# Attention with a bucket mask on one core: query parts of 256 and 512 columns instead of two of 384

## The chip, the core and the metric

The kernel runs on one core of a Trainium2 chip. The core has five engines with queues of their own: TensorE (PE; its weight loads are shown apart, as PEld), VectorE (DVE), ScalarE (ACT), GpSimd (POOL) and SyncE (SP), which here only issues DMAs. The metric is the time on the device in microseconds, as the median of the runs of one comparison.

## What is computed

The first half is attention over 4 batches, 8 heads, 768 positions and 64 values a head, in which a query sees only the keys that fall into its own bucket. The bucket comes from the signs of six projections. The second half is a gated MLP over the joined heads.

```
q_bits = (einsum('bhsd,dk->bhsk', q, proj) > 0)       # k_bits in the same way
mask = q_bucket[:, :, :, None] == k_bucket[:, :, None, :]
scores = where(mask, scale * q @ k.T, -1e9)
scores = scores - max(scores, -1)
attn = exp(scores); attn = attn / (sum(attn, -1) + 1e-9)
x = attn @ v                                          # (4, 768, 512) after joining the heads
h = gelu(x @ w_in); u, v = halves of h; v_n = layer norm of v * g_ln
out = x + (u * (w_sg @ v_n + b_sg)) @ w_out
```

## The kernel before

**Pairs of heads.** Two heads share the 128 partitions, 64 each, so there are 16 pairs. A matmul over one head's 64 rows uses half of TensorE's array, and the two heads' matmuls stand next to each other in the queue and run side by side; I call two such matmuls a row pair. The 768 queries of a pair are taken in two parts of 384, the 768 keys in six tiles of 128.

**The steps of a pair**, by the name of the function and the lines of the profile:

- `load` brings q, k and v by DMAs from SP.
- `parts` (L475 to L482): TensorE transposes 12 tiles, ScalarE rounds the result to the high part (L479; the queries are scaled here), VectorE takes the low part (L482).
- `features` (L497, L500): three matmuls for 384 columns give the projections, VectorE turns them into large signed constants that make the mask in a matmul.
- `largest` (L517, L524): for a tile of 128 queries and half of the keys a rough score, two row pairs of matmuls, and on VectorE the maximum over 384 keys for each head.
- `shift` (L532 to L545): the maxima of a part become one row of the features: VectorE, a spread over TensorE (L539), two ScalarE copies.
- `weigh` (L561, L567, L573, L582): for a tile of keys four row pairs give the scores of 384 queries (high x high, low x high, high x low, features), ScalarE takes the exponential; after every second key tile comes the product with v (four matmuls of 64 columns, two heads side by side); the exponentials are added up on GpSimd, and on VectorE for one key tile of five.
- `finish` (L598 to L621): the sums over keys by matmuls with ones in four strips of 32 columns, a reciprocal by way of DRAM, the scaling (L619) and the store into `xs`.

The product reads p with one more column of ones, 385 in all, which gives the sum of v. Scores, rough scores, transposes, features, spreads and totals all use the same seven PSUM tiles of one bank, `g0` to `g6`; the product has the eighth bank, `av`. A tile is free again when its readers are done.

**Weights.** Beside the attention, 16 jobs (`weight_job`, L326 to L365) split w_in into a high and a low part: per job one DMA, one GpSimd and one ScalarE operation, and seven on VectorE (L356 to L365).

**The order.** A planner (`Plan`) decides the order before the program is built: every group of instructions has an engine, a cost and a due number (`prio`), and the planner gives each engine the due group that can start earliest. The numbers at the top set these: `AVP` how late a product with v is due after its scores, `AHEAD` how many steps the rough scores are ahead, `WSTEP` and `WP` the distance and start of the weight jobs, `PREP` the start of the next pair's preparation. A pair takes 12 due numbers:

```
p0 = 12 * (n - 1) + PREP
weight_job(plan, w_tile, *job, WSTEP * i + WP)
plan.add(PE, 1.48, prio + AVP, product, p[0] + p[1] + [st.v], [av], form="col")
work = g["c"] + (self.TURN_PE if g["form"] != form else 0.0)
```

The form is the shape in which TensorE's array is used: "row" (64 rows, L517 and L561), "col" (64 columns, L573), 32 columns (L598), or the whole array. The MLP after it (L762, L790, L808, L834) uses the whole array throughout.

Of the kernel before, what the change touches and what calls it, by code (L numbers as in the profile page):

```python
# [21 lines left out]
MLP = {"xl": "POOL", "gm": "DVE", "gl": "POOL", "wg": 398.29, "wo": 46.93, "x": 568.79}  # L22

AVP = 4.5
NAV = 1
S0P = 2.08
AHEAD = 5
PREP, SHIFTP, FINP, WSTEP, WP = -2.61, 0.3, 5.42, 11, 9.29
LOADS = "SP"
ADDS = ["POOL", "POOL", "DVE", "POOL", "POOL"]  # L30


class Plan:
# [8 lines left out]
    TURN_PE = 0.09  # L42
    LANES = 8
    TURN = 4.7

# [56 lines left out]
    def order(self):  # L102
# [32 lines left out]
        while len(out) < len(G):  # L135
# [87 lines left out]
def kernel(  # L223
# [19 lines left out]
    P = 128  # L243
# [13 lines left out]
    MISS = 2.0 ** 33  # L257
    EMPTY = 2.0 ** 32
# [4 lines left out]
    QH2, W6 = SH // 2, SH // 64  # L263
# [12 lines left out]
    nc.vector.memset(ones, 1.0)  # L276
    less = const.tile([P, 1], F32, name="less")
# [36 lines left out]
    msts = [const.tile([P, HT, P], F32R, name=f"m{i}") for i in range(2)]  # L314
    for m in msts:
        nc.vector.memset(m.bitcast(F32), 0.0)
# [100 lines left out]
    if True:  # L417
# [30 lines left out]
        def load(n, prio):
# [11 lines left out]
            st.hi, st.lo, st.ft = ([pool.ring([P, S], F32R, f"{a}{c}{n % 3}") for c in "qk"] for a in ("h", "l", "f"))  # L460
# [5 lines left out]
        def parts(st, s, prio):  # L466

            hh, lo, raw, fac = st.hi[s], st.lo[s], st.raw[s], (SCALE, 1.0)[s]
            for hf in range(2):
                tp = ps_tile()  # L470
                cs = slice(hf * SH, (hf + 1) * SH)

                def tr(tp=tp, hf=hf):
                    for i in range(HT):
                        nc.tensor.transpose(tp()[:, i * P:(i + 1) * P],  # L475
                                            raw()[:, hf * HT + i].rearrange("p j d -> p (j d)"), ident)

                def high(tp=tp, cs=cs):
                    nc.scalar.mul(hh()[:, cs], tp()[:, :SH], fac)  # L479

                def low(tp=tp, cs=cs):
                    nc.vector.scalar_tensor_tensor(lo()[:, cs], tp()[:, :SH], fac, hh()[:, cs].bitcast(F32),  # L482
                                                   op0=ALU.mult, op1=ALU.subtract)

                plan.add(PE, 0.38, prio, tr, [raw, (hh, hf), (lo, hf)], [tp])
                plan.add(ACT, 0.49, prio, high, [tp], [(hh, hf)])
                plan.add(DVE, 0.55, prio, low, [tp, (hh, hf)], [(lo, hf)])

        def features(st, s, prio):
            hh, lo, ft = st.hi[s], st.lo[s], st.ft[s]  # L490
            for hf in range(2):
                cs = slice(hf * SH, (hf + 1) * SH)
                fp = ps_tile()

                def project(fp=fp, cs=cs):
                    for i, (w, x) in enumerate(((pwh, hh), (pwl, hh), (pwh, lo))):
                        nc.tensor.matmul(fp()[:, :SH], w[:, s, :], x()[:, cs], start=(i == 0), stop=(i == 2))  # L497

                def sign(fp=fp, cs=cs):
                    nc.vector.tensor_scalar(ft()[:, cs], fp()[:, :SH], fcol[:, 2 * s:2 * s + 1],  # L500
                                            fcol[:, 2 * s + 1:2 * s + 2], op0=ALU.is_gt, op1=ALU.mult)

                plan.add(PE, 0.58, prio, project, [(hh, hf), (lo, hf), (ft, hf)], [fp])
                plan.add(DVE, 0.67, prio, sign, [fp], [(ft, hf)])

        def largest(st, t, prio):

            hf, i = divmod(t, HT)
            if i == 0:
                st.mx = late.ring([P, 2, HT, 2], F32, "mx", 3)  # L510
            mx, qs = st.mx, slice(t * P, (t + 1) * P)
            sc = [[ps_tile() for j in range(2)] for kh in range(2)]

            def mm(kh):
                for n, x in enumerate((st.ft, st.hi)):
                    for j in range(2):
# [11 lines left out]
        def shift(st, hf, prio):  # L528
# [8 lines left out]
            def spread():  # L537
                for i in range(HT):
                    nc.tensor.matmul(tp()[:, i * P:(i + 1) * P], m()[:, i, :], identr, start=True, stop=True)  # L539
# [351 lines left out]
```

## Time and profile before

| | |
|---|---|
| median of three runs | 809.66 us (808.55 to 814.48) |
| the profiled execution | 808.19 us, span 806.4 us |
| attention, first to last matmul | about 5 to 480 us |
| MLP | about 481 to 806 us |
| granted TensorE clock | 0.998 of full speed |

The span is what the profile covers; the execution's own time has 1.8 us around it. In the rows a start is in microseconds from the start of the span. A timeline row gives the start, the length, the engine, the line, the operation, output and inputs, shapes, and how many instructions it merges; since matmuls are pipelined, the distance of two starts says what a matmul costs, and its length doesn't. A group row ends with count, busy time, mean length in ns, and the idle time before the group with what ended it. The chain is the work that ended last, followed back.

### The profile page before, as it was taken

To read this page: it belongs to the slowest core of one execution; us is meant where nothing else is said; L and a number is where in the kernel's file an instruction comes from. 1 tells how busy PE (TensorE), PEld (TensorE's weight loads), DVE (VectorE), ACT (ScalarE), POOL (GpSimd) and SP (SyncE) were. 2 spreads that over 40 slices of the span, in tenths; PEclk is the share of its full clock that TensorE was granted. 3 is DMA by queue.
4 is the path that set the end of the run, shared out by engine and by line. 5 is a ranking of instruction groups with operands and counts; after the bars stand their busy time and mean duration, and the time that the engine had idled before them with its cause. 6 is when DMAs were issued, how large, how long until landed. Compare 5 with 4: busy or idle time off the path is not lost.

```text
span 806.4 us, 14979 instructions
## 1 busy us (share of the span) xinstructions
PE 787.3 (98%) x5480; PEld 606.8 (75%) x5480; DVE 520.7 (65%) x1137; ACT 384.1 (48%) x863; POOL 387.1 (48%) x398
## 2 busy tenths in 40 slices
PE   7999999999999999999989999899999999999998
PEld 5776666666666666666656658898899889988996
DVE  7988888788878879798789645689124141405130
ACT  2566665655655665566556665623232133213211
POOL 0556666666675575676565885333015112501030
PEclk9999999999999999999999999999999999999999
DMA  6132232223313214313221124620402310040003
GB/s 150 34 83 61 67 101 70 80 78 90 83 64 102 74 52 102 73 53 101 73 64 51 31 79 137 225 80 26 153 5 79 105 52 26 15 131 27 1 1 130
DMA packets 98537, 60.65 MB, mean 75 GB/s; under 512 B 64672, under 2 KB 89376, under 8 KB 98464
## 3 DMA queue, kind: packets, MB, share of 16 engines
q1 hardware_dynamic: 96768, 56.94, 24.6%
q10 hardware_dynamic: 1696, 2.76, 1.0%
q8 instruction: 43, 0.70, 0.4%
q14 instruction: 30, 0.25, 0.1%
HBM read 46.90 MB, written 12.78 MB: 74 GB/s over the span
## 4 chain that ended last, share of the span: by engine, by line
PE 88%; DVE 7%; DMA 2%; POOL 1%; issue 1%; ACT 1%; SPq 0%; DVEq 0%; POOLq 0%; ACTq 0%
PE g L561 17%; PE av L573 15%; PE ps_vs L808 12%; PE ps_o L834 8%; PE g L517 8%; PE ps_h L790 8%; PE ps_h L762 7%; PE g L497 4%; PE g L475 3%; DVE mx L524 3%; PE g L539 2%; PE g L598 1%; PE ps_o L839 1%; DMA q<-in_q_dram 1%; POOL xl L697 1%
## 5 line engine op out<-in xcount | busy, mean ns | idle before, releaser
L582 POOL TENSOR_TENSOR sum<-sum,p 128x384 f32<-128x384 f32 x192 | 196.7, 1046 | 109.7 <-ACT p L567 95.8
L524 DVE TENSOR_REDUCE mx<-g 128x1 f32<-128x384 f32 x384 | 189.1, 549 | 54.4 <-PE g L517 53.8
L567 ACT ACTIVATE p<-g 128x384 f32<-128x384 f32 x384 | 160.4, 495 | 125.0 <-PE g L561 121.6
L573 PE MATMUL av<-p,v 128*64 128x385 f32 x768 | 144.9, 499 | 0.0
L573 PEld LDWEIGHTS av<-p,v 128*64 128x64 f32 x768 | 46.7, 136 | 57.7 <-issue 57.0
L561 PE MATMUL g<-hq,hk 64*128 64x384 f32 x384 | 78.9, 389 | 1.7 <-DVE mx L524 1.5
L517 PE MATMUL g<-fk,fq 64*128 64x384 f32 x384 | 73.3, 352 | 3.6 <-DVE mx L524 3.3
L582 POOL TENSOR_TENSOR sum<-p,p 128x384 f32<-128x384 f32 x64 | 64.2, 1023 | 25.7 <-ACT p L567 25.6
L811 DVE SCALAR_TENSOR_TENSOR gt<-ps_vs,g_col,b_bc 128x384 f32<-128x384 f32 x32 | 19.7, 616 | 79.9 <-PE ps_vs L808 79.8
L561 PEld LDWEIGHTS g<-hq,hk 64*128 64x128 f32 x384 | 38.3, 183 | 43.1 <-issue 22.3
L517 PE MATMUL g<-hk,hq 64*128 64x384 f32 x384 | 68.8, 336 | 0.0
L561 PE MATMUL g<-hq,lk 64*128 64x384 f32 x384 | 67.7, 335 | 0.0
L561 PE MATMUL g<-fq,fk 64*128 64x384 f32 x384 | 67.4, 333 | 0.0
L561 PE MATMUL g<-lq,hk 64*128 64x384 f32 x384 | 67.4, 334 | 0.0
L819 POOL TENSOR_TENSOR gs<-gt,gs 128x384 fp32r<-128x384 f32 x32 | 33.0, 1030 | 70.7 <-ACT gs L816 70.5
L834 PE MATMUL ps_o<-woh,gs 128*128 128x512 f32 x192 | 65.5, 402 | 0.0
L808 PE MATMUL ps_vs<-wgh,zh 128*128 128x384 f32 x192 | 64.2, 334 | 0.0
L808 PE MATMUL ps_vs<-wgh,zl 128*128 128x384 f32 x192 | 64.2, 334 | 0.0
L808 PE MATMUL ps_vs<-wgl,zh 128*128 128x384 f32 x192 | 64.1, 334 | 0.0
L773 POOL TENSOR_TENSOR mv<-mv,epsr 128x1 f32<-128x1 f32 x24 | 16.3, 679 | 99.5 <-DVE mv L772 99.5
L770 DVE BATCH_NORM_STATS2 st<-y 128x6 f32<-128x512 f32 x24 | 16.6, 690 | 67.7 <-ACT y L751 67.7
L517 PEld LDWEIGHTS g<-fk,fq 64*128 64x128 f32 x384 | 39.9, 184 | 18.7 <-DVE mx L524 11.2
(125 smaller groups left out, 1621.1 us busy)
## 6 DMA issues: line engine op xcount, KB each, us to landing
q<-in_q_dram SPq DMA_DIRECT2D x32, 192.0 KB, 3.7
k<-in_k_dram SPq DMA_DIRECT2D x32, 192.0 KB, 3.7
v<-in_v_dram SPq DMA_DIRECT2D x16, 384.0 KB, 3.3
rs<-r SPq DMA_DIRECT2D x64, 96.0 KB, 2.9
xs<-xt SPq DMA_DIRECT2D x32, 192.0 KB, 2.2
x<-xs SPq DMA_DIRECT2D x16, 384.0 KB, 2.9
rx<-xs SPq DMA_DIRECT2D x96, 64.0 KB, 1.9
out_dram<-ob SPq DMA_DIRECT2D x24, 256.0 KB
```

The source lines that it names most:

```text
L497: nc.tensor.matmul(fp()[:, :SH], w[:, s, :], x()[:, cs], start=(i == 0), stop=(i == 2))
L517: nc.tensor.matmul(sc[kh][j]()[:, :SH], x[0]()[row(j), qs], x[1]()[row(j), kh * SH:(kh + 1) * SH], start=(n == 0), stop=(n == 1))
L524: plan.add(DVE, 0.56, prio, lambda j=j, kh=kh: nc.vector.tensor_reduce(mx()[:, kh, i, j:j + 1], sc[kh][j]()[:, :SH], axis=AX.X, op=ALU.max ...
L561: nc.tensor.matmul(sc[i][j]()[:, :SH], x()[row(j), ks], y()[row(j), cs], start=(n == 0), stop=(n == 3))
L567: plan.add(ACT, 0.53, prio, lambda i=i, j=j: nc.scalar.activation(p[i][j]()[:, :SH], sc[i][j]()[:, :SH], AF.Exp), [sc[i][j]], [p[i][j]])
L573: nc.tensor.matmul(av()[row(j), :SH + 1], st.v()[:, j, kt, :], p[i][j](), start=(kt == 0), stop=(kt == NT - 1))
L582: (nc.gpsimd if e == POOL else nc.vector).tensor_add(sums[j](), first()[:, :SH], p[i][j]()[:, :SH])
L762: nc.tensor.matmul(ps(), x()[:, ts_], w[:, c, FH:FF], start=(c == 0 and n == 0), stop=(c == NC - 1 and n == 2))
L790: nc.tensor.matmul(ps()[:, :SH], w[:, c, fs], x()[:, cs], start=(c == 0 and n == 0), stop=(c == NC - 1 and n == 2))
L808: nc.tensor.matmul(vp(), z()[:, t, fs], w()[:, t, cs], start=(t == 0 and n == 0), stop=(t == NT - 1 and n == 2))
L819: nc.gpsimd if e == POOL else nc.vector).tensor_sub(gl()[:, cs], gt(), gh()[:, cs].bitcast(F32)),
L834: nc.tensor.matmul(po(), a()[:, ts_], w()[:, f, :], start=(f == 0 and n == 0), stop=False)
```

## The change

The queries of a pair are taken in a part of 256 and a part of 512. In the first part (`ph` 0) a PSUM tile holds two key tiles by 256 queries, in the second (`ph` 1) one key tile by 512 queries, so that every tile of scores fills its bank; a pair has nine such steps (`NU`) instead of twelve. The rough scores come in nine steps too: 128 queries by 512 keys, and 2 x 128 queries by the last 256 keys. Transposes and features come in three chunks instead of four. The exponential applies the scale (the queries are no longer scaled, and the constants of the mask grow by 8). Products with v come in groups of one and two steps (`GY`) and of three and three (`GX`). In `finish`, the small constant is added on ScalarE with the copy of the sums and not on VectorE (L608 before), the scaling moves to GpSimd, and the addition of the mean of v to VectorE, in one operation with its factor. The planner now has a cost for each change of form (`TURNS`) and prefers to stay in a form (`STAY`); a pair takes 18 due numbers; and most due numbers are new. Cut to its core:

```diff
-MLP = {"xl": "POOL", "gm": "DVE", "gl": "POOL", "wg": 398.29, "wo": 46.93, "x": 568.79}
-AVP = 4.5
+MLP = {"xl": "POOL", "gm": "DVE", "gl": "POOL", "wg": 209.05, "wo": 46.93, "x": 568.79}
+AVP = 4.99
+GY, GX, NPT = (1, 2), (3, 3), 16
-AHEAD = 5
-PREP, SHIFTP, FINP, WSTEP, WP = -2.61, 0.3, 5.42, 11, 9.29
+AHEAD = 8
+PREP, SHIFTP, FINP, WSTEP, WP = -3.85, 0.3, 6.08, 12.04, 25.31
-ADDS = ["POOL", "POOL", "DVE", "POOL", "POOL"]
+ADDS = (["POOL", "POOL"], ["POOL", "POOL", "DVE", "POOL", "POOL"])
...
-    TURN_PE = 0.09
+    TURNS = {"row": 0.2, "col": 0.144, "full": 0.17, "c32": 0.1, None: 0.0}
+    STAY = 2.0
...
+            def rank(n):
+                return G[n]["p"] + (self.STAY if e == "PE" and G[n]["form"] != form else 0.0), n
...
-    QH2, W6 = SH // 2, SH // 64
+    NY = S // 3
+    PHASES = ((0, NY), (NY, S))
+    WIDE = 2 * NY
...
-                    nc.scalar.mul(hh()[:, cs], tp()[:, :SH], fac)
+                nc.scalar.copy(hh()[:, ss, cs], at(tp))
...
+            def mm():
+                for c, t in enumerate(tiles):
+                    qs = slice((t0 + t) * P, (t0 + t + 1) * P)
+                    for n, x in enumerate((st.ft, st.hi)):
+                        for j in range(2):
+                            nc.tensor.matmul(sc[j]()[:, c * NY:c * NY + b - a], x()[row(j), 0, qs], x()[row(j), 1, a:b],
+                                             start=(n == 0), stop=(n == 1))
...
+            kts = (2 * u, 2 * u + 1) if ph == 0 else (u,)
...
+            def mm():
+                for i, kt in enumerate(kts):
+                    ks = slice(kt * P, (kt + 1) * P)
+                    for m, (x, y) in enumerate(((hi, hi), (lo, hi), (hi, lo), (ft, ft))):
+                        for j in range(2):
+                            nc.tensor.matmul(sc[j]()[:, i * w:(i + 1) * w], x()[row(j), 1, ks], y()[row(j), 0, cs], start=(m == 0), stop=(m == 3))
...
-                    plan.add(ACT, 0.53, prio, lambda i=i, j=j: nc.scalar.activation(p[i][j]()[:, :SH], sc[i][j]()[:, :SH], AF.Exp),
+                plan.add(ACT, 0.6, prio, lambda j=j: nc.scalar.activation(p[j]()[:, :, :NY], two(sc[j]()), AF.Exp, scale=SCALE),
...
+                def product():
+                    for x in us:
+                        for j in range(2):
+                            if ph == 1:
+                                nc.tensor.matmul(two(av())[row(j)], st.v()[:, j, x, :], ps[x][j]()[:, :, :NY], start=(x == 0), stop=(x == 5))
+                        for i in range(2 - 2 * ph):
+                            for j in range(2):
+                                nc.tensor.matmul(av()[row(j), :NY + 1], st.v()[:, j, 2 * x + i, :], ps[x][j]()[:, i, :],
+                                                 start=(x == 0 and i == 0), stop=(x == 2 and i == 1))
...
+            def total():
+                for i in range(2 - ph):
+                    for j in range(2):
+                        for a in range(2):
+                            r, c = 64 * j + 32 * a, i * NY + a * h
+                            nc.tensor.matmul(tp()[r:r + 32, :h], ones, sums[j]()[:, c:c + h], start=(i == 0), stop=(i == 1 - ph))
...
-            plan.add(DVE, 0.16, prio, lambda: V.tensor_single_scalar(sq(), sq(), 1e-9, op=ALU.add), [sq], [sq], port=True)
...
-            plan.add(ACT, 0.62, prio, lambda: nc.scalar.mul(e(), e(), vm()[:, 0:1]), [e, vm], [e])
-            plan.add(DVE, 0.56, prio, lambda: V.tensor_mul(xt(), un()[:, :SH], rs()), [un, rs], [xt], port=True)
-            plan.add(POOL, 0.98, prio, lambda: nc.gpsimd.tensor_add(xt(), xt(), e()), [xt, e], [xt])
+            plan.add(POOL, 0.13 + n / 420.0, prio + TAILP, lambda: nc.gpsimd.tensor_mul(xt()[:, :n], un()[:, :n], rs()[:, :n]), [un, rs], [xt])
+            plan.add(DVE, 0.1 + n / 960.0, prio + TAILP, lambda: V.scalar_tensor_tensor(
+                xt()[:, :n], e()[:, :n], vm()[:, 0:1], xt()[:, :n], op0=ALU.mult, op1=ALU.add), [xt, e, vm], [xt], port=True)
...
-            p0 = 12 * (n - 1) + PREP
+            p0 = 2 * NU * (n - 1) + PREP
```

The order that comes out is read from the built program, engine by engine (the lists that the prediction counts in). On TensorE, before, a product with v of four matmuls stands between row pairs (L517 rough scores, L561 scores; `g` are PSUM tiles, `h`, `l` and `f` the high part, low part and features of q and k):

```order
L517 MATMUL g_960_3472<-hk_2_2907,hq_2_2880 128x384
L517 MATMUL g_960_3474<-hk_2_2907,hq_2_2880 128x384
L573 MATMUL av_3427<-p_153,v_2689 64x385
L573 MATMUL av_3427<-p_154,v_2689 64x385
L573 MATMUL av_3427<-p_155,v_2689 64x385
L573 MATMUL av_3427<-p_156,v_2689 64x385
L561 MATMUL g_960_3495<-hq_2_2880,hk_2_2907 128x384
L561 MATMUL g_960_3497<-hq_2_2880,hk_2_2907 128x384
```

Of the change, at the same stage of a pair (L608 the product, L494 transposes, L565 the spread, L514 features):

```order
L494 MATMUL g_736_2706<-ident,q_2337 128x128 x4
L608 MATMUL av_2714<-p_163,v_2103 64x512
L608 MATMUL av_2714<-p_164,v_2103 64x512
L608 MATMUL av_2714<-p_165,v_2103 64x512
L608 MATMUL av_2714<-p_166,v_2103 64x512
L608 MATMUL av_2714<-p_157,v_2103 64x512
L608 MATMUL av_2714<-p_158,v_2103 64x512
L565 MATMUL g_736_2738<-identr,m_151 128x128 x2
L514 MATMUL g_736_2744<-h_2_2703,pwh 128x256
```

Three steps' products stand together, and they stand beside work of the whole array.

On VectorE, before, a weight job (`w`, `wx`, `wy`, `wg` are its tiles) is strewn between maxima (L524, `mx`):

```order
L365 SCALAR_TENSOR_TENSOR wil<-wx_2295,wih 128x256
L356 TENSOR_SCALAR wy_2727<-w_6_2658 128x256
L357 SCALAR_TENSOR_TENSOR wx_2729<-w_6_2658,wy_2727 128x256
L524 TENSOR_REDUCE mx_2745<-g_960_2732 128x1
L524 TENSOR_REDUCE mx_2745<-g_960_2734 128x1
L524 TENSOR_REDUCE mx_2745<-g_960_2753 128x1
L524 TENSOR_REDUCE mx_2745<-g_960_2755 128x1
L619 TENSOR_TENSOR xt_2788<-un_2440,rs_2676 128x384
L359 SCALAR_TENSOR_TENSOR wx_2729<-wg_2748,wx_2729 128x256
```

Of the change, in a pair with weight work (the lines of the job are seven higher, the maxima are L547):

```order
L363 TENSOR_SCALAR wy_2889<-w_8_2570 128x256
L364 SCALAR_TENSOR_TENSOR wx_2891<-w_8_2570,wy_2889 128x256
L366 SCALAR_TENSOR_TENSOR wx_2891<-wg_2615,wx_2891 128x256
L368 TENSOR_SCALAR wy_2889<-wx_2891 128x256
L369 SCALAR_TENSOR_TENSOR wy_2889<-w_8_2570,wy_2889 128x256
L370 TENSOR_TENSOR wx_2891<-wx_2891,wy_2889 128x256
L547 TENSOR_REDUCE mx_2931<-g_736_2916 128x1
L547 TENSOR_REDUCE mx_2931<-g_736_2918 128x1
L547 TENSOR_REDUCE mx_2931<-g_736_2923 128x1
L547 TENSOR_REDUCE mx_2931<-g_736_2925 128x1
```

Six operations of one job stand in a row ahead of four maxima.

More of the change, by code (lines that the diff above doesn't have):

```diff
@@ L464, in load @@
             return st
[L466 to L487, printed above, removed]
@@ L528, in shift, with chunk, parts, at @@
-        def shift(st, hf, prio):
+        def chunk(i):
+            (a, b), (c, d) = PHASES
+            return ((slice(0, 2), slice(a, b), [(0, 0), (1, 0)]), (1, slice(c, d), [(1, 1)]), (0, slice(c, d), [(0, 1)]))[i]
+        def parts(st, i, prio):
+            hh, lo, (ss, cs, keys), tp = st.hi, st.lo, chunk(i), ps_tile()
+            def at(t):
+                return two(t()) if i == 0 else t()[:, :WIDE]
+            def tr():
+                c = 0
+                for s, _ in keys:
+                    for t in range(cs.start // P, cs.stop // P):
+                        nc.tensor.transpose(tp()[:, c:c + P], st.raw[s]()[:, t].rearrange("p j d -> p (j d)"), ident)
+                        c += P
+            def high():
+                nc.scalar.copy(hh()[:, ss, cs], at(tp))
+            def low():
+                nc.vector.tensor_sub(lo()[:, ss, cs], at(tp), hh()[:, ss, cs].bitcast(F32))
+            plan.add(PE, 0.48, prio, tr, [st.raw[s] for s, _ in keys] + [(t, x) for t in (hh, lo) for x in keys], [tp], form="full")
+            plan.add(ACT, 0.6, prio, high, [tp], [(hh, x) for x in keys])
+            plan.add(DVE, 0.69, prio, low, [tp] + [(hh, x) for x in keys], [(lo, x) for x in keys])
@@ L570, in product @@
-            def product():
-                for i, kt in enumerate(two):
-                    for j in range(2):
-                        nc.tensor.matmul(av()[row(j), :SH + 1], st.v()[:, j, kt, :], p[i][j](), start=(kt == 0), stop=(kt == NT - 1))
-            plan.add(PE, 1.48, prio + AVP, product, p[0] + p[1] + [st.v], [av], form="col")
-            for i, kt in enumerate(two):
-                if kt == 0:
-                    continue
-                e = ADDS[kt - 1]
-                for j in range(2):
-                    def add(j=j, i=i, e=e, first=p[0][j] if kt == 1 else sums[j]):
-                        (nc.gpsimd if e == POOL else nc.vector).tensor_add(sums[j](), first()[:, :SH], p[i][j]()[:, :SH])
-                    plan.add(e, 1.01 if e == POOL else 0.55, prio + 0.6, add, [p[i][j]] + ([p[0][j]] if kt == 1 else []),
+            sc, p = [ps_tile() for j in range(2)], [p_tile() for j in range(2)]
@@ L585, in weigh, with add, finish @@
+            if u:
+                e = ADDS[ph][u - 1]
+                for j in range(2):
+                    def add(j=j, e=e, first=st.p[0][j] if u == 1 else sums[j]):
+                        a = first()[:, :, :NY] if u == 1 else two(first())
+                        (nc.gpsimd if e == POOL else nc.vector).tensor_add(two(sums[j]()), a, p[j]()[:, :, :NY])
+                    plan.add(e, 1.35 if e == POOL else 0.62, prio + 0.6, add, [p[j]] + ([st.p[0][j]] if u == 1 else []),
                              [sums[j]], port=True)
-        def finish(st, hf, prio):
+        def finish(st, ph, prio):
@@ L592, in finish @@
             V = nc.vector
             def total():
-                for j in range(2):
-                    for a in range(2):
-                        r = 64 * j + 32 * a
-                        nc.tensor.matmul(tp()[r:r + 32, :QH2], ones, sums[j]()[:, a * QH2:(a + 1) * QH2], start=True, stop=True)
-            plan.add(PE, 0.6, prio, total, sums, [tp])
-            plan.add(ACT, 0.32, prio, lambda: nc.scalar.copy(sm(), tp()[:, :QH2]), [tp], [sm])
-            un = late.ring([P, SH + 1], F32, "un", 3)
@@ new lines, in finish @@
+            plan.add(PE, 0.5, prio, total, sums, [tp], form="c32")
+            plan.add(ACT, 0.25 + h / 1400.0, prio, lambda: nc.scalar.activation(sm()[:, :h], tp()[:, :h], AF.Identity, bias=small[:, 0:1]), [tp], [sm])
+            un = late.ring([P, WIDE], F32, "un", 3)
+            m = n + 1 - ph
+            plan.add(ACT, 0.22 + m / 1400.0, prio - 1, lambda: nc.scalar.copy(un()[:, :m], av()[:, :m]), [av], [un])
+            sd, sb = dram.tile([4, h], F32, name=f"s_{st.n}_{ph}"), plan.buf(f"s_{st.n}_{ph}", 1)
@@ L625 @@
+        NPAIR, NU = B * NP, 9
         sts = {}
```

200 lines of the change are left out of this document (105 added, 95 removed).

## The prediction

> **What bounds the kernel now.** I read the page's totals first, then the chain that ended last, then that chain in order of time, then TensorE's timeline inside one period.
>
> ```profile
> span 806.4 us, 14979 instructions
> PE 787.3 (98%) x5480; PEld 606.8 (75%) x5480; DVE 520.7 (65%) x1137; ACT 384.1 (48%) x863; POOL 387.1 (48%) x398
> PE 88%; DVE 7%; DMA 2%; POOL 1%; issue 1%; ACT 1%; SPq 0%; DVEq 0%; POOLq 0%; ACTq 0%
> ```
>
> TensorE carries 88% of the chain. A busy TensorE isn't one at its peak, so the question is what fills its time. The chain in order of time answers it:
>
> ```profile
> 101.59 1.79 PE g L497 x9
> ...
> 246.23 1.79 PE g L497 x9
> ...
> 394.26 0.73 PE g L497 x3
> ...
> 427.25 1.76 PE g L497 x9
> ```
>
> The features of the next pair (L497) come back pair by pair: 101.59 to 246.23 is five pairs, 144.64 us or 28.93 each. In that stretch the chain has TensorE pieces only, so 28.93 us is what one pair costs TensorE there. From 246.23 to 427.25 six pairs take 181.02 instead of 173.58, so 7.4 us were lost to something else. The window from 100 to 200 us shows how near the others are (busy time of TensorE, its weight loads, VectorE, ScalarE, GpSimd, with counts; then the clock):
>
> ```profile
> 100.00:200.00 100.00, 100.00 (x821) 67.62 (x819) 82.59 (x182) 60.58 (x147) 63.08 (x65) 1.00 0.30 81
> ```
>
> The clock column is 1.00, so the throttle plays no part.
>
> **Inside a period.** TensorE's timeline around one product with v:
>
> ```profile
> 250.20 0.35 PE L517 MATMUL g<-hk,hq 64*128 64x384 f32 x2
> 250.48 1.51 PE L573 MATMUL av<-p,v 128*64 128x385 f32 x8
> 251.92 0.44 PE L561 MATMUL g<-hq,hk 64*128 64x384 f32 x2
> 252.20 0.34 PE L561 MATMUL g<-hq,lk 64*128 64x384 f32 x2
> 252.37 0.34 PE L561 MATMUL g<-lq,hk 64*128 64x384 f32 x2
> ...
> 259.42 0.53 PE L598 MATMUL g<-sum,ones 128*32 128x192 f32 x8
> 259.88 0.44 PE L561 MATMUL g<-hq,hk 64*128 64x384 f32 x2
> ...
> 273.27 0.55 PE L539 MATMUL g<-identr,m 128*128 128x128 f32 x3
> 273.66 0.84 PE L475 MATMUL g<-ident,k 128*128 128x128 f32 x6
> 274.43 0.44 PE L561 MATMUL g<-hq,hk 64*128 64x384 f32 x2
> ```
>
> A pair of row-tiled matmuls (two heads side by side) starts 0.17 us after the one before (252.20 to 252.37; 0.174 over longer runs). Across a change of shape (64 rows, 64 columns, 32 columns, full array; I call it a turn) it is 0.28 from 250.20 to 250.48 and again from 251.92 to 252.20, 0.11 lost each time. The product itself takes 1.44 for 8 records, while a long one shows what its stream needs:
>
> ```profile
> 475.68 4.10 PE L573 MATMUL av<-p,v 128*64 128x385 f32 x24
> ```
>
> The 16 further records cost 4.10 - 1.51 = 2.59, 0.162 each, so 8 need 1.30, and 0.14 more is lost. One product between two row stretches thus loses 0.11 + 0.14 + 0.11 = 0.36, or **0.18 a turn**. The period gives the same from the other side: 48 + 24 row pairs and 12 features at 0.174 are 14.6, 48 product records at 0.162 are 7.8, 12 transposes at 0.128 (273.66 to 274.43) 1.5, 6 spreads at 0.13 (273.27 to 273.66) 0.8, two totals at 0.35 (0.46 less one gap) 0.7: together 25.4. The 3.5 left of 28.93 fall on the 22 turns that the list of a period has: **0.16 a turn**.
>
> **The change part by part.** *Turns.* Over the whole attention the lists have 326 changes of shape before and 220 now. The title says five products with v; the list shows three stretches of 64 columns in a steady pair, where six stood. 106 turns x 0.16 = **-17.0 us**; with 0.18, -19.1, with the bare gap 0.11, -11.7. Number and total columns of scores, maxima, features, transposes, spreads and products stay.
>
> *Widths.* Half of the 384-wide matmuls become 256 wide, half 512. Two 512-wide rows of the MLP:
>
> ```profile
> 485.16 0.39 PE L762 MATMUL ps_h<-wih,xh 128*128 128x512 f32 x1
> 485.39 0.40 PE L762 MATMUL ps_h<-wil,xh 128*128 128x512 f32 x1
> ```
>
> 0.23 for 512 and 0.174 for 384 is 0.45 ns a column in both, so 256 columns should take 0.116 and nothing changes. The other bound is the 128-wide spread at 0.13, which costs far more than its columns: if no issue goes under 0.13, the 672 issues of 256 columns (24 + 12 + 6 in a pair, 16 pairs) add 672 x 0.014 = 9.4. What lies under it are the weight loads:
>
> ```profile
> 260.86 0.19 PEld L561 LDWEIGHTS g<-lq,hk 64*128 64x128 f32 x2
> ...
> 273.27 0.41 PEld L539 LDWEIGHTS g<-identr,m 128*128 128x128 f32 x3 [0.30 <-ACT hq L479]
> ```
>
> Two half-height loads together take 0.19, no more than one, and three full ones 0.41, so a further load costs (0.41 - 0.19) / 2 = 0.11, just under 0.116. I take **+2**, bounds 0 and +9.4. The Trainium skill (TensorE: Matmul & The Clock Gate, LDWEIGHTS) says that a load takes columns / 1.2 ns whatever the rows, an estimate of 107 ns here. By that rule this term would be 0 and the time 2 us less; the 0.11 of the trace agrees.
>
> *Totals (L598).* 2 x 192 columns become 256 + 2 x 128: 0.7 x 512/384 = 0.93, +0.23 in each of 16 pairs, **+3.7**. They wait for nothing that they didn't wait for before.
>
> *VectorE, and the 7.4 us.* The stall at 284 us in the chain:
>
> ```profile
> 284.40 1.94 DVE mx L524 x4
> 286.35 0.54 DVE wy L356
> ...
> 287.90 1.04 DVE wy L361
> 288.94 0.48 DVE mx L524
> ```
>
> Maxima stand in VectorE's queue behind a weight job (L356 to L365), their PSUM tiles stay taken, and TensorE waits for a tile. In a pair, 24 maxima become 18. Twelve of them took 5.66 in a row, 0.47 each:
>
> ```profile
> 14.12 5.66 DVE L524 TENSOR_REDUCE mx<-g 128x1 f32<-128x384 f32 x12 [0.20 <-PE g L517]
> ...
> L524 DVE TENSOR_REDUCE mx<-g 128x1 f32<-128x384 f32 x384 | 189.1, 549 | 54.4 <-PE g L517 53.8
> L770 DVE BATCH_NORM_STATS2 st<-y 128x6 f32<-128x512 f32 x24 | 16.6, 690 | 67.7 <-ACT y L751 67.7
> L608 DVE TENSOR_SCALAR sq<-sq 128x6 f32<-128x6 f32 x32 | 15.9, 498 | 4.5 <-DMA sq<-s 4.5
> L582 DVE TENSOR_TENSOR sum<-sum,p 128x384 f32<-128x384 f32 x64 | 33.7, 566 | 3.9 <-POOL sum L582 3.6 <-ACT sm L601 0.3
> ```
>
> By the nearest 512-wide row, 0.14 longer than a 384-wide one, a new maximum takes 0.61: 11.0 a pair against 11.3. L608 goes (15.9 / 16 = 1.0), four adds become two of 0.7 (2.1 to 1.4): VectorE loses about 2 us of its 23.9 a pair (82.59 in 100 us). But the weight jobs are put 12.04 apart where a pair takes 18 steps, not 11 in 12: 1.5 jobs a pair instead of 1.1. A job is seven operations of 0.3 to 1.0, about 4 us, so +1.6 a pair until the jobs are done in the 12th; afterwards there are none. So it comes out lighter, but not by much while the jobs last. I take half of the stalls, **-3.5**, bounds 0 and -7.4.
>
> *Start and end.* The first shift waits for 6 maxima of 0.61 instead of 12 of 0.47, 2 us earlier; TensorE still owes the other maxima, so **-1** (0 to -2). At the end the last part has four adds for each head on GpSimd:
>
> ```profile
> L582 POOL TENSOR_TENSOR sum<-sum,p 128x384 f32<-128x384 f32 x192 | 196.7, 1046 | 109.7 <-ACT p L567 95.8 <-DVE sum L582 7.3 <-DVE lk L482 4.2
> L697 POOL TENSOR_TENSOR xl<-x,xh 128x768 fp32r<-128x768 f32 x16 | 30.4, 1913 | 39.4 <-ACT xh L699 39.4
> ```
>
> Between 1.05 and 1.91 a 512-wide add is 1.33; eight and a VectorE pair are 12 us beside about 13 of TensorE's scores and products, and they start 2 to 3 us later: **+1** (0 to +2). GpSimd has 12 adds of 1.33 a pair for 16 of 1.04, so nothing there. ScalarE loses instructions and has 40% idle. The MLP's list for TensorE is the same row for row, including the place of the gate's weights: 0.
>
> **Sum:** -17.0 + 2 + 3.7 - 3.5 - 1 + 1 = -14.8. The profiled execution took 808.19 for its span of 806.4, 1.5 under the median of 809.66; so the span goes to 791.6 and the median to **794.9 us**.
>
> **Rivals.**
> (a) *VectorE takes over (slower).* For ten pairs the weight jobs come 1.5 to a pair, and the new list has six of a job's operations in a row ahead of four maxima, each holding one of seven PSUM tiles, now full banks. The worst period before, by the chain from 394.26 to 427.25, lost 4.06 us. Without my 3.5 for stalls the gain is 11.3. If ten pairs lose L each and the 7.4 go, the change turns to a loss when 10 L exceeds 18.7, at 1.9 a pair; at 3 a pair it is 809.66 - 11.3 - 7.4 + 30 = 821. For it stands L361, 1.04 above (minimum, median and maximum in ns):
>
> ```profile
> L361 DVE TENSOR_SCALAR wy<-wx x16: 279/289/1104, 26.2 to 436.7; 128x256 int32<-128x256 int32 x16
> ```
>
> VectorE already waits there, up to 0.8 us, most of one of GpSimd's adds, and those adds grow by 0.29. Against: VectorE's load falls and TensorE is ahead by more maxima. The Trainium skill (SBUF — State Buffer, Who interferes with whom) says that a VectorE instruction with two SBUF inputs, or in a two-port mode, and a GpSimd instruction exclude each other for the whole instruction. The 1.04 agrees. 10%.
> (b) *Short streams are bound by their loads*, 0.13 for every 256-wide issue: 7.4 more, 802.3. For it the spread's row, against it the paired loads. 12%.
> (c) *The turns go, but their time returns as a wait*, since products now come late and in lumps and the totals wait for GpSimd's sums: 2.2 above today, 811.9. Against it stand GpSimd's 63% and ScalarE's 61% of busy time. 5%.
> (d) *More*: 0.18 a turn and no stalls, 809.66 - 19.1 + 2 + 3.7 - 7.4 - 1 + 1 = 788.9, or less. 13%.
>
> **How the numbers follow.** My case has 60%, and nearly all of it, with (d) and a third of (b), is faster by over 1%, which is about what this measurement can tell from no change (below 801.6): 0.74. Within 1%: the rest of (b), (c) and the edge of mine, 0.16. Slower: 0.10. All low ends together are -19.1 + 3.7 - 7.4 - 2 = -24.8, 784.9; all high ends -11.7 + 9.4 + 3.7 + 2 = +3.4. The range, 785 to 806, leaves out (a) and little else.
>
> **What would show it.** The features' rows should recur every 27.7 to 28.1 us in steady pairs; a product of six matmuls should be followed at once; 256-wide row pairs should start 0.116 to 0.12 apart (0.13 is (b)); the chain between pairs 9 and 15 should hold fewer VectorE pieces. A period above 28.9 with VectorE or ScalarE pieces in it proves me wrong.

## The result: 818.4 us, one per cent slower

| | before | after |
|---|---|---|
| median, 17 runs each | 809.66 us (805.39 to 814.48) | 818.43 us (812.33 to 821.24) |
| ratio, with its 95% interval | | 1.0103 [1.0083, 1.0124] |
| the profiled execution | 808.19 us, span 806.4 | 820.94 us, span 818.8 |
| first matmul of the MLP, start | 481.56 | 493.02 |

The forecast was 794.9 us, 785 to 806. The change made the kernel slower, and it did so before the MLP: there TensorE begins 11.5 us later, and the span is 12.4 us longer. (The two profiled executions lie 2.5 us above and 1.5 below their medians, so they differ by 4 us more than the medians do.) The page of the profile after, in its totals and in the shares of the chain:

```profile
span 818.8 us, 14669 instructions
...
PE 782.7 (96%) x5608; PEld 599.2 (73%) x5608; DVE 539.0 (66%) x962; ACT 359.6 (44%) x703; POOL 370.6 (45%) x334
...
PE 74%; DVE 19%; DMA 2%; issue 2%; ACT 2%; SPq 0%; POOL 0%; ACTq 0%; DVEq 0%
```

TensorE's share of the chain fell from 88% to 74%, VectorE's rose from 7% to 19%, and VectorE is busy 18.3 us longer (539.0 for 520.7) with 175 instructions fewer. The features' rows of the chain in order of time (start, length) tell where:

```profile
102.81 2.31 PE g L514 x12
...
385.55 2.31 PE g L514 x12
...
413.26 2.17 PE g L514 x12
...
441.59 2.31 PE g L514 x12
```

From 102.81 to 385.55 lie nine pairs, 282.74 us or **31.4 each**, where the forecast had 27.7 to 28.1 and the kernel before 28.93. The two pairs behind them, in which no weight job is left, take 27.71 and 28.33, about the forecast's. Against 28.0 the nine lose 3.4 each, 31 us in all.

The same pairs by windows, first of before and then of after (busy time of TensorE, its loads, VectorE, ScalarE and GpSimd with counts; the granted clock; DMA share and GB/s):

```profile
217.30:246.23 28.93, 28.93 (x239) 19.38 (x239) 23.13 (x53) 17.74 (x44) 18.61 (x19) 1.00 0.28 79
```

```profile
195.74:225.73 29.99, 28.38 (x247) 18.50 (x246) 27.81 (x47) 17.27 (x35) 18.43 (x16) 1.00 0.27 73
...
256.98:290.06 33.08, 29.73 (x247) 19.34 (x247) 28.09 (x44) 16.71 (x34) 19.03 (x17) 0.95 0.28 76
...
385.55:413.26 27.71, 27.71 (x247) 18.75 (x248) 20.32 (x35) 15.16 (x30) 16.84 (x14) 1.00 0.31 81
```

VectorE goes from 23.13 to about 28 us a pair with fewer instructions, and TensorE stands still for 1.6 and 3.4 us in the first two. In the second the clock is 0.95 as well. Over all nine pairs, by the same view, TensorE stands still for 19.5 us; most of the rest of the 31 goes with the clock (last section).

### The profile page after: what moved, and what is told of

Same layout as the page of the kernel before. It is cut to its first block, busy times and chain, and to the rows that moved or that the text cites. A ratio compares the mean times of both kernels' runs of the same rounds, so it can differ in the third digit from the quotient of the medians.

```text
span 818.8 us, 14669 instructions
## 1 busy us (share of the span) xinstructions
PE 782.7 (96%) x5608; PEld 599.2 (73%) x5608; DVE 539.0 (66%) x962; ACT 359.6 (44%) x703; POOL 370.6 (45%) x334
## 4 chain that ended last, share of the span: by engine, by line
PE 74%; DVE 19%; DMA 2%; issue 2%; ACT 2%; SPq 0%; POOL 0%; ACTq 0%; DVEq 0%
PE g L593 14%; PE ps_vs L852 11%; PE ps_o L878 8%; PE g L539 7%; PE av L608 7%; PE ps_h L806 7%; PE ps_h L834 6%; PE g L514 4%; PE av L611 4%; PE g L494 3%; DVE m L559 3%; DVE mx L547 2%; DVE mx L549 2%; DVE mx L558 2%; DVE xt L663 1%
## 5 line engine op out<-in xcount | busy, mean ns | idle before, releaser
L598 ACT ACTIVATE p<-g 128x512 f32<-128x512 f32 x288 | 155.7, 600 | 102.5 <-PE g L593 101.7
L620 POOL TENSOR_TENSOR sum<-sum,p 128x512 f32<-128x512 f32 x128 | 159.3, 1264 | 55.9 <-DVE sum L620 32.0
L547 DVE TENSOR_REDUCE mx<-g 128x1 f32<-128x512 f32 x192 | 121.7, 679 | 21.3 <-PE g L539 18.6
L620 POOL TENSOR_TENSOR sum<-p,p 128x512 f32<-128x512 f32 x64 | 85.4, 1354 | 87.4 <-ACT p L598 87.4
L608 PE MATMUL av<-p,v 128*64 128x512 f32 x384 | 89.6, 602 | 0.0
L593 PE MATMUL g<-h 64*128 64x256 f32 (+1 forms) x384 | 76.3, 360 | 5.6 <-DVE mx L547 4.9
L549 DVE TENSOR_REDUCE mx<-g 128x2 f32<-128x512 f32 x96 | 61.9, 684 | 23.9 <-PE g L539 22.0
L539 PE MATMUL g<-f 64*128 64x256 f32 (+1 forms) x384 | 73.2, 366 | 0.8 <-DVE f L519 0.5
L593 PE MATMUL g<-h,l 64*128 64x256 f32 (+1 forms) x384 | 72.1, 342 | 0.0
L593 PE MATMUL g<-l,h 64*128 64x256 f32 (+1 forms) x384 | 71.0, 339 | 0.0
L593 PE MATMUL g<-f 64*128 64x256 f32 (+1 forms) x384 | 70.9, 338 | 0.0
L539 PE MATMUL g<-h 64*128 64x256 f32 (+1 forms) x384 | 68.3, 342 | 0.0
L608 PEld LDWEIGHTS av<-p,v 128*64 128x64 f32 x384 | 24.9, 137 | 43.8 <-issue 41.8
```

Of the source, the lines that this page charges most:

```text
L539: nc.tensor.matmul(sc[j]()[:, c * NY:c * NY + b - a], x()[row(j), 0, qs], x()[row(j), 1, a:b], start=(n == 0), stop=(n == 1))
L547: nc.vector.tensor_reduce(mx()[:, 0, i0 + w, j:j + 1], sc[j]()[:, :WIDE], axis=AX.X, op=ALU.max, negate=True)
L549: nc.vector.tensor_reduce(mx()[:, 1, i0:i0 + 2, j], two(sc[j]()), axis=AX.X, op=ALU.max, negate=True)
L593: nc.tensor.matmul(sc[j]()[:, i * w:(i + 1) * w], x()[row(j), 1, ks], y()[row(j), 0, cs], start=(m == 0), stop=(m == 3))
L598: plan.add(ACT, 0.6, prio, lambda j=j: nc.scalar.activation(p[j]()[:, :, :NY], two(sc[j]()), AF.Exp, scale=SCALE), [sc[j]], [p[j]])
L608: nc.tensor.matmul(two(av())[row(j)], st.v()[:, j, x, :], ps[x][j]()[:, :, :NY], start=(x == 0), stop=(x == 5))
```

## Where the time goes in a pair

I take the pair with 33.08 us. TensorE's timeline (start, length; in brackets the idle time and what ended it), around the spread L565 that turns the shift's row:

```profile
264.59 2.80 PE L608 MATMUL av<-p,v 128*64 128x512 f32 x12
267.32 0.64 PE L640 MATMUL g<-sum,ones 128*32 128x256 f32 x8
270.48 0.63 PE L565 MATMUL g<-identr,m 128*128 128x128 f32 x4 [2.52 <-DVE m L559]
271.04 0.59 PE L539 MATMUL g<-f 64*128 64x512 f32 x2
271.43 0.63 PE L539 MATMUL g<-h 64*128 64x512 f32 x2
```

TensorE waits 2.52 us for `m`, the result of L559. Over the whole trace the view of waits puts 15.7 us in 17 places to this line, the largest that TensorE has for another engine; next come 4.9 us for maxima (L547), which stand behind the shift and the weight work on VectorE. In that stretch VectorE does this:

```profile
265.71 1.57 DVE L369 SCALAR_TENSOR_TENSOR wy<-w,wy 128x256 f32<-128x256 uint32 x1
267.31 0.81 DVE L370 TENSOR_TENSOR wx<-wx,wy 128x256 f32<-128x256 f32 x1
268.05 1.14 DVE L558 TENSOR_TENSOR mx<-mx 128x8 f32<-128x8 f32 x1
269.22 1.11 DVE L559 SCALAR_TENSOR_TENSOR m<-mx 128x8 fp32r<-128x8 f32 x1
```

L558 and L559 are the shift: eight numbers in each partition, and over 1.1 us each. GpSimd at the same time:

```profile
263.95 2.97 POOL L620 TENSOR_TENSOR sum<-p,p 128x512 f32<-128x512 f32 x2 [0.36 <-ACT p L598]
266.88 0.96 POOL L662 TENSOR_TENSOR xt<-un,rs 128x256 f32<-128x256 f32 x1
267.81 2.49 POOL L620 TENSOR_TENSOR sum<-sum,p 128x512 f32<-128x512 f32 x2
```

The pair of additions that starts at 267.81 ends at 270.30, and L559 ends at 270.33. One addition takes about 1.25, so the first ends near 269.1, where L558 ends (269.19). L558 and L559 have both inputs in SBUF, and each is done when an addition of GpSimd is done. The Trainium skill (SBUF — State Buffer, Who interferes with whom) describes it: a VectorE instruction with two SBUF inputs and a GpSimd instruction that reads SBUF exclude each other for the whole instruction. The trace agrees, and shows what a short instruction pays. The groups of VectorE after (count, busy time, mean ns):

```profile
L559 DVE SCALAR_TENSOR_TENSOR m<-mx 128x8 fp32r<-128x8 f32 x16 | 15.2, 952 | 0.6
L558 DVE TENSOR_TENSOR mx<-mx 128x8 f32<-128x8 f32 x16 | 15.2, 950 | 0.1
L559 DVE SCALAR_TENSOR_TENSOR m<-mx 128x4 fp32r<-128x4 f32 x16 | 15.0, 937 | 0.5
...
L558 DVE TENSOR_TENSOR mx<-mx 128x4 f32<-128x4 f32 x16 | 5.3, 329 | 0.5
```

64 instructions cost 50.7 us. Before, by line (minimum, median and maximum in ns):

```profile
L532 DVE TENSOR_TENSOR mx<-mx x32: 124/166/851, 19.8 to 463.6; 128x6 f32<-128x6 f32 x32
...
L533 DVE SCALAR_TENSOR_TENSOR m<-mx x32: 169/170/175, 20.0 to 463.8; 128x6 fp32r<-128x6 f32 x32
```

L533, the twin of L559, never waited: 0.17 us at all 32 places. L532, the twin of L558, stayed within 0.23 us at 30 places and took 0.57 and 0.85 at the other two. At 0.18 each the 64 would be 11.5 us, so 39 us of waiting came into VectorE's queue. Why L533 never waited, VectorE's timeline before shows, and then GpSimd's:

```profile
260.13 0.22 DVE L532 TENSOR_TENSOR mx<-mx 128x6 f32<-128x6 f32 x1
260.38 0.17 DVE L533 SCALAR_TENSOR_TENSOR m<-mx 128x6 fp32r<-128x6 f32 x1
260.46 1.02 DVE L582 TENSOR_TENSOR sum<-sum,p 128x384 f32<-128x384 f32 x2
```

```profile
257.37 1.97 POOL L582 TENSOR_TENSOR sum<-sum,p 128x384 f32<-128x384 f32 x2 [1.08 <-ACT p L567]
259.71 0.61 POOL L358 TENSOR_TENSOR wg<-w 128x256 f32<-128x256 f32 x1 [0.36 <-DMA w<-in_moe_w_in_dram]
261.51 1.05 POOL L582 TENSOR_TENSOR sum<-sum,p 128x384 f32<-128x384 f32 x1 [1.18 <-DVE sum L582]
```

There the shift stands directly ahead of VectorE's own additions L582, and GpSimd's next addition waits for those (1.18 us idle). The shift fell into a gap that its own queue made. In the new order it stands amid weight work, while GpSimd has its additions in a row.

## The experiments

Two theories stood after this reading. A: the shift's two operations wait for GpSimd's additions, and TensorE waits for the shift. B: the weight jobs, six of their operations in a row, hold up the maxima, and so the PSUM tiles. Each expectation says what its theories make of the run. The ratio is always to the kernel before on the same chip.

### The shift as one reduction (e1), and the same in the kernel before (e4)

`mx` gets a third plane that holds the limit; one `tensor_reduce` takes the minimum of the three. A reduction has one input. What changes in the computation: a query whose bucket holds no key gets the limit (2 to the 35th) as its shift, where it got zero. Nothing else moves on any queue.

```diff
...
-            plan.add(DVE, 0.16, prio, lambda: V.tensor_tensor(mx()[:, 0, :nt], mx()[:, 0, :nt], mx()[:, 1, :nt], op=ALU.min), ...
-            plan.add(DVE, 0.16, prio, lambda: V.scalar_tensor_tensor(
-                m()[:, :nt, MROW::BL], mx()[:, 0, :nt], EMPTY, mx()[:, 0, :nt], op0=ALU.is_lt, op1=ALU.mult),
+            plan.add(DVE, 0.16, prio, lambda: V.tensor_reduce(
+                m()[:, :nt, MROW::BL], mx()[:, :, :nt].rearrange("p k a b -> p a b k"), axis=AX.X, op=ALU.min),
```

> The changed kernel, with the two small VectorE operations of the shift (two inputs in SBUF each) replaced by one reduction over the two maxima and a constant, one input in SBUF; all queues keep their order. Theory A (the shift's two operations wait for GpSimd's adds, 39 us of VectorE's time over the kernel beyond the 0.17 to 0.2 us they need, and TensorE waits behind them): the new operation takes 0.2 to 0.3 us, never 0.9, and of the 30 us that the pairs with weight work lose at least half comes back: 798 to 804 us. Theory B (the weight jobs' mass and their lumps of six in VectorE's queue are the cause): the shift is quick but the periods stay near 31 us, 812 to 818 us.

> The kernel before, with the shift as one reduction as in the first of these runs. Its two operations took 0.17 to 0.2 us each at the median, so both theories expect no change: 806 to 811 us. A gain of over 1% would mean that the one reduction helps for another reason than the wait for GpSimd.

e1 took 797.5 us, 0.9857 [0.9827, 0.9886]: 20 us less than the change as it was. e4 took 811.2, 1.0018 [0.9996, 1.004]: in the old order, where the shift hardly waits, the same edit gives nothing. In e1's groups:

```profile
L564 DVE TENSOR_REDUCE m<-mx 128x8 fp32r<-128x24 f32 x16 | 2.8, 172 | 0.1
L564 DVE TENSOR_REDUCE m<-mx 128x4 fp32r<-128x12 f32 x16 | 2.7, 168 | 0.5
```

The reduction takes 0.17 beside the same additions, with three times as many elements. The Trainium skill (SBUF — State Buffer, Who interferes with whom) says that this instruction never contends on this chip, and the trace agrees. Ten pairs of e1 take 29.0 us each (features at 101.45 and 391.91). That is still 1 us above the forecast: the additions now meet the weight work instead, L364 takes 1.035 us on average where it took 0.646, L363 0.909 for 0.540.

### Without the weight work: e2, and with the reduction e8

The seven VectorE operations of each w_in job are left out, and ScalarE fills the weights with a constant; TensorE's list is unchanged.

```diff
...
-            plan.add("DVE", 0.07 + CW / 960.0, when(), fn, r, wr, port=True)
+            plan.add("DVE", 0.07 + CW / 960.0, when(), (lambda: None) if th is wih else fn, r, wr, port=True)
...
```

> The changed kernel without the seven VectorE operations of each of w_in's 16 weight jobs: ScalarE fills the weights with a constant instead, so the weights are left out of the computation; TensorE's queue is the same row for row. Theory B: every period falls to the 27.7 to 28.3 us of the pairs that had no weight work, about 790 us. Theory A alone (the shift waits all the same): periods stay above 29.5 us, 803 us or more. Both needed together: about 790 us here too.

> The changed kernel with the shift as one reduction and without the VectorE operations of w_in's weight jobs (the weights are left out of the computation, as in the second run). It shows what is left when both are gone: TensorE's own time, 16 periods of 27.7 to 28.0 us and the start, 785 to 789 us. At 792 us the shift's waits would cost nothing where there is no weight work.

| ratio to before | shift as it was | shift as one reduction |
|---|---|---|
| with weight work | 1.0103 | 0.9857 (e1) |
| without | 0.9789 (e2) | 0.9647 (e8) |

e2 took 792.1 us, e8 782.8. By differences of ratios, times 809.66: the shift's waits cost 20 us beside the weight work and 11.5 without; the weight work costs 25 us beside the waits and 17 without, each good to about 3 us. Both theories hold a part, and 8.4 us, give or take 4, belong to neither alone. That fits a VectorE without slack when both are there, but it isn't shown, and the clock is a rival: in the profiled executions its mean was 0.987 with both, 0.993 in e1, 0.999 in e2 and 1.0 in e8, up to 10.6, 5.6, 0.8 and 0 us, which could make 4 of the 8.4. In e2 the shift's operations still take 0.84 to 0.94 us (0.25 for the first of the 128x4), so taking the weight work away doesn't shorten most of them; it leaves VectorE time to bear them, and TensorE waits for the shift 5.3 us in 12 places for 15.7 in 17. e8, under the 785 to 789 that I expected, is what TensorE needs by itself. Its chain, features, and the window from 100 to 400 us:

```profile
100.43 2.28 PE g L524 x12
128.06 2.27 PE g L524 x12
```

```profile
100.00:400.00 300.00, 300.00 (x2680) 201.99 (x2680) 202.85 (x357) 180.64 (x371) 193.01 (x164) 1.00 0.32 83
```

TensorE is busy for 300.00 of 300 us, and a pair takes 27.63.

### The jobs further apart: e3, and with the reduction e5

```diff
-PREP, SHIFTP, FINP, WSTEP, WP = -3.85, 0.3, 6.08, 12.04, 25.31
+PREP, SHIFTP, FINP, WSTEP, WP = -3.85, 0.3, 6.08, 16.5, 13.9
```

> The changed kernel with the weight jobs spread over nearly all pairs, as before the change (16.5 due numbers apart instead of 12.04, 1.09 jobs a pair instead of 1.5). Theory B: VectorE is under its limit in every pair, periods of 28.0 to 28.8 us, 796 to 804 us. Theory A: the waits come back in the pairs that had none, the loss is spread and not removed, 812 to 820 us.

> The changed kernel with the shift as one reduction and with the weight jobs spread over nearly all pairs. The shift is worth 21 us alone, the spread 10 alone. If both act by the same limit (VectorE late for TensorE), together they end near what no weight work gives: 789 to 796 us. If the spread only moved the shift's waits about, it adds nothing to the reduction: 797 to 800 us.

e3 took 807.8 us, 0.9979 [0.9965, 0.9992], between the two expectations: 10 us came back. But the edit also moved the shift against the additions (the 128x8 form of L558 fell from 0.950 to 0.680 us, the 128x4 form of L559 from 0.937 to 0.837; all 64 take 45.9 us for 50.7), so it doesn't tell the theories apart. e5 does: 799.4, 0.9847 [0.9814, 0.988], no better than e1. Once the shift is free of waits, the distance of the jobs gives nothing that can be measured.

### GpSimd's additions in halves: e6, with the reduction e9, in the kernel before e10

The shift stays as it was; each addition of 512 columns on GpSimd is issued as two of 256. The work is the same, and a waiting VectorE instruction gets its turn after half the time.

```diff
-                        (nc.gpsimd if e == POOL else nc.vector).tensor_add(two(sums[j]()), a, p[j]()[:, :, :NY])
+                        if e == POOL:
+                            for h in range(2):
+                                nc.gpsimd.tensor_add(two(sums[j]())[:, h], a[:, h], p[j]()[:, h, :NY])
+                        else:
+                            nc.vector.tensor_add(two(sums[j]()), a, p[j]()[:, :, :NY])
```

> The changed kernel with the shift as it was and each of GpSimd's adds of 512 columns issued as two of 256 (about 0.74 us each, so GpSimd has some 1.8 us more a pair). If VectorE's operation waits for the one add that runs when it comes, the shift's two operations fall from 0.9 and 1.1 us at the median to about 0.5, and a third to a half of the 21 us comes back: 807 to 812 us. If it waits until GpSimd has no add left, they stay as long and the time stays at 816 to 822 us.

> The changed kernel with both repairs: the shift as one reduction that waits for no addition (797.5 by itself) and GpSimd's additions of 512 columns issued as two of 256 (798.3 by itself). Theory A (two victims of the same waits, the shift and the weight work: the reduction repairs only the first, the halved additions shorten both): 789 to 794, weight operations L364 and L366 faster than the 1035 and about 1200 ns that they took with the reduction alone. Theory B (the halved additions gained only through the shift, so the two repairs are the same one): 796 to 799.

> The kernel before, with GpSimd's additions of 384 columns issued as two of 192; nothing else. Theory A (before, the shift never meets an addition, and only weight operations wait for one now and then): 806 to 811, no change that matters. Theory B (shorter additions help any order of this kernel, so that the 20 us that they gave the changed kernel say nothing of the change): 795 to 802.

e6 took 798.3 us, 0.984 [0.9812, 0.9868], more than expected. Its groups, VectorE's two and GpSimd's one:

```profile
L559 DVE SCALAR_TENSOR_TENSOR m<-mx 128x8 fp32r<-128x8 f32 x16 | 10.5, 654 | 0.6
...
L622 POOL TENSOR_TENSOR sum<-sum,p 128x256 f32<-128x256 f32 x256 | 180.4, 736 | 39.5 <-DVE sum L624 19.7
```

A half takes 0.74 us for 1.26 of a whole, so GpSimd is busy 33 us longer (403.9 for 370.6), and the kernel is 20 us faster. The engine was made slower and the time fell: what counted was how long one instruction keeps the others out. The granted clock rose with it, from 0.987 to 0.999, so up to 10 of the 20 us can have come by way of the clock.

e9 took **787.4 us**, 0.9733 [0.9704, 0.9761], the fastest version that does all the work, just under A's 789 to 794. Its features stand at 101.71 and, ten pairs later, at 380.34:

```profile
101.71 2.28 PE g L518 x12
...
380.34 2.16 PE g L518 x12
```

27.86 us a pair, inside the forecast. The two repairs add up, since they help different instructions: L364 is back at 0.685 us, L363 at 0.586. (L366 took 0.741 on average in e1, not the 1.2 of the expectation, and 0.647 here.)

e10 took 803.1, 0.9922 [0.989, 0.9954]: between the expectations, and A's "no change that matters" was wrong. The steady pairs are as before, 28.93 (features from 102.52 to 247.15). The six pairs behind them took 181.02 and now 176.04:

```profile
247.15 1.79 PE g L497 x9
...
423.19 1.76 PE g L497 x9
```

So 5.0 of the 7.4 us that the prediction had counted as stalls of the kernel before go with shorter additions; the operations that became faster are those of the weights (L357 went from 0.853 to 0.678 us). The shift doesn't stay free here: L533 now takes 0.52 at nine places, 0.27 on average, and the steady pairs bear it. The fairest price of the change itself is then e9 against e10, both with short additions and a shift that delays TensorE little: 0.9733 / 0.9922 = 0.981, 15 us.

### The old kernel made to wait: e11

If the place keeps the shift of the old order free, taking the gap away should bring the loss into the kernel before. VectorE's additions go to GpSimd; so VectorE has less to do. The planner then puts all queues in another order too, TensorE's with 15 changes of form fewer.

```diff
-ADDS = ["POOL", "POOL", "DVE", "POOL", "POOL"]
+ADDS = ["POOL", "POOL", "POOL", "POOL", "POOL"]
```

> The kernel before, with the key tile whose additions stood on VectorE (L582, four of 20 a pair) given to GpSimd like the others: VectorE loses 2.1 us a pair, GpSimd rises from 18.6 to about 22.8 of 28.93, and the gap goes in which GpSimd waited for VectorE's addition, just where the shift's two operations stood. Theory A (it was that place, not the 384 columns, that kept the shift free of waits): L532 and L533 rise from 0.17 to 0.4 us or more on average, weight operations too, and the time goes to 813 to 824. Theory B (additions of 384 columns are too short to matter): L532 and L533 stay under 0.3, and the time is 804 to 811.

823.6 us, 1.0156 [1.0122, 1.019], about as slow as the change or slower. The shift's second line, by the same view as before:

```profile
L533 DVE SCALAR_TENSOR_TENSOR m<-mx x32: 169/909/944, 20.1 to 476.5; 128x6 fp32r<-128x6 f32 x32
```

The median rose from 170 to 909 ns, and TensorE waits for L533 12.4 us in 18 places, where it waited 0.8 in two. VectorE's timeline, and then GpSimd's, in the place where the gap was:

```profile
247.94 0.92 DVE L532 TENSOR_TENSOR mx<-mx 128x6 f32<-128x6 f32 x1
248.90 0.92 DVE L533 SCALAR_TENSOR_TENSOR m<-mx 128x6 fp32r<-128x6 f32 x1
```

```profile
245.90 3.89 POOL L582 TENSOR_TENSOR sum<-sum,p 128x384 f32<-128x384 f32 x4 [0.61 <-ACT p L567]
249.75 0.61 POOL L358 TENSOR_TENSOR wg<-w 128x256 f32<-128x256 f32 x1
```

Four additions of 0.97 end at 249.79; the shift's two are done at 248.86 and 249.82, with the third and the fourth. So the loss needs no wider additions: 384 columns are long enough, and the place decides whether it occurs; the length (e6) sets its size. GpSimd also carries 4 additions a pair more here (view of windows, 100 to 400 us: 224.55 busy for 190.35), and its order moved; how much of the loss belongs to these, this run doesn't separate.

### The price of a turn: e7

The reduction of e1, but the products with v one step at a time and no preference for staying in a shape: 422 turns instead of 220, everything else of the change kept.

```diff
-GY, GX, NPT = (1, 2), (3, 3), 16
+GY, GX, NPT = (1, 1, 1), (1, 1, 1, 1, 1, 1), 16
...
-    STAY = 2.0
+    STAY = 0.0
```

> The changed kernel with the shift as one reduction, with a product with v for every step (1, 1, 1 and six times 1) and without the preference to stay in a form: 422 changes of form in TensorE's list instead of 220. At 0.16 us a turn that is 32 us; VectorE gets more time in a pair and gives back up to 6 of the waits: 822 to 830 us, and a steady period of 29.8 to 30.2 us. If turns cost little and products were only waited for, 797 to 804 us.

828.5 us, 1.0208 [1.0174, 1.0242]. Against e1 that is 0.0351 x 809.66 = 28.4 us for 202 turns, 0.14 each, if nothing else cost time. But e1 has waits that longer pairs can absorb. A pair without weight work takes 30.0 here (features at 356.89 and, three pairs later, at 446.84) for 27.6 in e1 (364.23 to 419.46, two pairs) and in e8; by the matmuls' order that is 27 turns for 13 to 14, 0.17 to 0.18 each.

## Why the prediction was wrong, point by point

**The step that failed** is "VectorE, and the 7.4 us": -3.5, with bounds 0 and -7.4. The stalls of the pairs didn't fall from 7.4 us to 3.9; they rose to 31, so the term measured about +23.6 in the profiled executions. With that in its place the sum gives +12.3, and the span grew by 12.4: the other terms, taken together, came out as forecast. (By the medians, which differ by 8.8, it is about +20.) All high ends of the sum together reach 813.1 and the stated range stopped at 806; the result lies beyond both. The sum for VectorE was made of durations as they stood in the trace before, "VectorE loses about 2 us of its 23.9 a pair", and a duration there held whatever waiting the old order gave. The two operations of the shift weren't costed at all: at 0.17 us they looked like nothing. They wait 0.6 us each on average in the new order, four a pair, 2.4 us in the one queue on which TensorE waits. Over the whole trace the shift takes 50.7 us of VectorE for 11.9 before; without these 39 us VectorE would have been busy 20 us less than before, and the forecast's "lighter" would have been right. The bound "0" had no reason behind it: in the trace of before L361 took 279 to 1104 ns, and L532, one of the shift's own two, 851 once for a median of 166, so what the moved operations would meet in their new places had to be asked. I had looked at the order for what stands behind the maxima, not for what GpSimd does beside the shift.

**Rival (a)** had the effect right: VectorE takes over, slower, about ten pairs, at 3 us a pair 821. It measured nine pairs at 3.4, and 818.4. It had the weight work in the place of the waits and quoted the rule of the exclusion, but set it against "VectorE's load falls", which is no argument against waits, and gave 10%. By e1, e2 and e8 it was both: 20 us hang on the shift's waits and 25 on the weight work, about 8 of them counted in both.

**Turns, -17.0:** right. The list of a steady pair has 14 turns now for 22. With the 25.4 of the prediction plus 0.1 for the widths and 0.23 for the totals, e8's 27.63 leaves 1.9 for 14 turns, 0.14 each; e7 gives 0.14 to 0.18, where I took 0.16. (The "five products" that the prediction reads in a title stand nowhere: `GY` and `GX` make four, in the three stretches that it counts.)

**Widths, +2:** right, and (b) is out. Row pairs of 256 columns in e9, in a stretch without waits:

```profile
135.27 0.28 PE L598 MATMUL g<-h,l 64*128 64x256 f32 x2
135.39 0.28 PE L598 MATMUL g<-l,h 64*128 64x256 f32 x2
135.51 0.28 PE L598 MATMUL g<-f 64*128 64x256 f32 x2
...
137.63 2.79 PE L613 MATMUL av<-p,v 128*64 128x512 f32 x12
140.36 0.66 PE L570 MATMUL g<-identr,m 128*128 128x128 f32 x4
```

They start 0.12 apart, and the product of six row pairs is followed at once, by the spread that in the change as it was had to wait.

**Totals, +3.7:** right. Two stretches a pair take 0.57 each to the next row in e9 (from 140.95 to 141.52 and from 149.37 to 149.94), where one took 0.46: +0.22 a pair.

**Start and end, -1 and +1:** not tested alone. The MLP, forecast at 0, takes 325.8 us for 324.8 before, from its first matmul to the end of the span.

**(c), the turn time returns as a wait:** not in its place. Products that come late and in lumps cost nothing in e8, where TensorE is busy without a break.

**(d), 788.9 or less:** with both repairs the change gets there (e9, 787.4), 7 us below my own sum. Up to 3.9 of the 7 are the other half of the old stalls, of which I had taken -3.5; where the rest is from wasn't tested. So the parts that I had costed came out near their price, and the one that I hadn't costed decided.

## What to carry to other kernels

A duration in a trace is work plus waiting, and a reordering changes the second part: before an instruction is carried at its old duration, ask what it could meet in its new place. Two places to ask are every VectorE instruction with two SBUF inputs, however small, and every GpSimd instruction that may run beside it; on a chain that TensorE waits for, one input (a reduction here) or shorter GpSimd instructions gave back 20 us each. If a change of order disappoints, compare the mean duration of the same operation before and after, smallest shapes first.

## What the runs showed of the hardware that I had not expected

An idle of TensorE can be paid again behind it. After the 2.52 us of waiting at 270.48 (nothing ran from 267.96 on), the windows of two us each read:

```profile
270.00:272.00 2.00, 1.52 (x10) 1.30 (x12) 0.66 (x2) 0.83 (x2) 0.91 (x2) 0.83 0.43 158
272.00:274.00 2.00, 2.00 (x12) 0.95 (x10) 1.91 (x4) 0.32 (x1) 0.00 (x0) 0.50 0.00 0
274.00:276.00 2.00, 2.00 (x15) 1.06 (x13) 1.60 (x4) 0.03 (x1) 0.00 (x0) 0.82 0.07 26
```

The granted clock falls to a half for 2 x (0.17 + 0.50 + 0.18) / 0.5 = 3.4 us, and row pairs of 512 columns start 0.42 apart (271.43 to 271.85 in the timeline) instead of 0.23. That is 1.7 us lost on top of 2.5. The Trainium skill (TensorE: Matmul & The Clock Gate, Part 1) says that the clock goes to half after an idle window of about 3.4 us and back after a busy one; the 3.4 of half speed agrees, but an idle of 2.5 us sufficed here. Four more pairs have such a stretch, behind idles of 2.73, 1.64, 1.63 and 2.29 us (from 125.63, 238.04, 312.68 and 373.08); behind one of 1.62 (from 335.41) the clock stays at 1.00, so the length of the idle alone doesn't decide. The five pairs with a clock of 0.90 or 0.95 in the windows (34.3 us at 0.90 and four of 31 to 33 at 0.95) lose up to 34.3 x 0.10 + 130.3 x 0.05 = 10 us by it, a third of the 31; with the 19.5 of standing still that is nearly all of it. The 17 executions of the change agree: the shortest, 812.3 us, had a mean clock of 0.996, the longest, 821.2, one of 0.987. In e6 and e9, whose waits are shorter, the clock is back at 0.999 and 0.997.

Halving GpSimd's additions made the old kernel faster too (e10), at 41 us more of GpSimd's time (428.2 busy for 387.1).
